# One fused attention and expert kernel: an order table with one place for each single operation, and 1e-9 brought in by a second small sum

## The chip, the cores and the metric

The kernel runs on one core of one Trainium2 chip. The metric is the device time of one execution in microseconds (us). TensorE (PE, with its weight loads PEld), VectorE (DVE), ScalarE (ACT), GpSimd (POOL) and the queue of SyncE (SP), which issues every DMA, run side by side. Each works off its own instructions in program order and waits where data or a buffer is not free.

## The reference

```python
# attention: 4 batches, 8 heads, 768 positions, 64 wide, chunks of 32 queries
scores = scale * np.matmul(q_c, k_full.transpose(0, 1, 3, 2))   # 56 keys around the chunk and 8 memory keys
scores = scores - np.max(scores, axis=-1, keepdims=True)
a = np.exp(scores)
a = a / (np.sum(a, axis=-1, keepdims=True) + 1e-09)
out[:, :, c_start:c_end] = np.matmul(a, v_full)
...
# x: (3072, 512) from the heads; w_in: 512 x 2048, w_out: 2048 x 512, handed in as float64
h = x @ w_in
P = a[0] + a[1] * h + a[2] * h2 + a[3] * h3
Q = 1.0 + np.abs(b[0]) * np.abs(h) + np.abs(b[1]) * h2
g = P / (Q + 1e-06)
return (g @ w_out).astype(np.float32)
```

## The kernel before

The 3072 tokens are six blocks of 512, and the 2048 hidden columns sixteen groups of 128. A **step** is one group of hidden columns for one block, so there are 96 steps. Each step n has a first product `g1(n)` (12 matmuls, three for each of four slices of x, because each fp32 factor is split into a high and a low part), a chain of elementwise operations on the 128x512 result h, and a second product `g2(n)` (12 matmuls into four output tiles). Steps 0 to 7 belong to block 0, steps 8 to 23 to block 1, steps 24 to 31 to block 0 again, and the blocks 2 to 5 follow. Two PSUM tiles hold h in turn, so `g1(n+2)` can start only when the chain of step n has read its h for the last time.

One letter stands for each operation in the order table. For a step: `g` first product; ACT's `s` (absolute value, then slope times it plus constant) and `i` (cubic's first line); POOL's `p` (product in the denominator); DVE's `j` (two operations, called j and J below); ACT's `t` (logarithm and exponential, t and T); DVE's `r` (three operations, r, R and Q; Q is the last to read h); POOL's `u` (high part) and `y` (low part, by a subtraction); `o` second product. For half of a weight group: `w` its DMA, ACT's `A`, DVE's `B` (a shift and a combining operation, B and C), ACT's `H` (high part), POOL's `L` (low part); 32 such halves are converted. For one of four head pairs of a block's attention: `b` scores, `m` maximum and subtraction, `x` exponential, `z` row sums, 1e-9 and reciprocal, `c` `k` transposition, `d` values, `n` division, `e` transposition back, `h` and `l` high and low part of x.

The first 31 steps, the conversion of all weights and the attention of blocks 0 to 2 stand in the string `SEQ`, written out by hand, and every engine keeps that order. Blocks 0 and 1 (`BLOCKWISE`) do their attention in PSUM tiles of 128x512 through TensorE; later blocks use a form with DVE's block transposition and DMAs. From step 31 on a loop sets the order. `RAW_SLOTS` says which piece of SBUF a weight's raw words are loaded into, `QK_SLOTS` and `V_SLOTS` which ones hold the first queries, keys and values; `CLEAR` says which engine zeroes which of these at the start; `XL_POOL` says which low parts of x POOL takes rather than DVE.

The addition of 1e-9 before the reciprocal is one DVE operation on 128x8 numbers, with a second operand `scaled` (a constant 256) in SBUF:

```python
pin(nc.vector.scalar_tensor_tensor(rinv, sums, 1e-9, scaled.broadcast_to([P, 2 * NG]), op0=ALU.add, op1=ALU.mult))
pin(nc.vector.reciprocal(rinv, rinv))
```

Of the kernel before, what the change touches and what calls it, by code (L numbers as in the profile page):

```python
# [45 lines left out]
ORDER = "i0 i1 o0 i2 i3 o1 i4 o2 i5 i6 o3 i7 o4 o5 o6 o7 i13 o13 i11 i9 i8 o8 o11 o9 i10 o10 i12 o12 i14 o14 i15 o15"  # L46
# [3 lines left out]
v02 H m03 L x03 v03 h00 Y W W d01 B l00 W c02 k02 c03 n01 w e01 z03 d02 q10 z02 n02 w k03 d03 e02 H L q11 h01 w f00  # L50
n03 A e03 l01 P h02 b10 f01 h03 A B l02 f02 w m10 B l03 f03 H x10 z10 b11 s i m11 c10 L A k10 f10 q12 j B f11 p H t
f12 r f13 v10 L x11 s u i q13 p b12 z11 c11 H k11 A g L b13 j m12 w t s w x12 A B m13 d10 p n10 i e10 v11 c12 x13 c13
r v12 H A d11 B k12 L y g w j n11 B h10 v13 H w t r d12 k13 s L e11 H d13 z12 h11 z13 l10 n12 g u A B p y i e12 A h12
w n13 j H L o t l11 w l12 w B r s L A w o B u p i w y H L A j u g B H t s L A r o w i H y g A p B j u t w s B L A y H
o p r e13 w B i g L H L j A t B w u s h13 i v21 r l13 y o j A B g p H A t r A s w i H L u j w B o g p t y r H u B A y
# [28 lines left out]
def attn_moe(ctx, tc, qk, vm, w, ab, out, seq):  # L84
# [678 lines left out]
```

## Time and profile before

| what | before |
|---|---|
| median of 3 runs | 611.65 us (611.23 to 613.16) |
| the profiled execution's own time | 611.78 us |
| its span, first to last instruction | 610.0 us |
| time outside the span | 1.78 us |
| PE busy | 587.4 us (96%) |
| DVE busy | 488.7 us (80%) |
| POOL busy | 418.2 us (69%) |
| ACT busy | 397.9 us (65%) |

The shares are means over a program whose parts differ: before about 90 us DVE and POOL are filled, after 300 us PE is. PE's granted clock is 1.00 in every stretch, which is the upper of its two levels (2.4 GHz).

### The profile page before, as it was taken

To read this page: it belongs to the slowest core of one execution; us is meant where nothing else is said; L and a number is where in the kernel's file an instruction comes from. 1 tells how busy PE (TensorE), PEld (TensorE's weight loads), DVE (VectorE), ACT (ScalarE), POOL (GpSimd) and SP (SyncE) were. 2 spreads that over 40 slices of the span, in tenths; PEclk is the share of its full clock that TensorE was granted. 3 is DMA by queue.
4 is the path that set the end of the run, shared out by engine and by line. 5 is a ranking of instruction groups with operands and counts; after the bars stand their busy time and mean duration, and the time that the engine had idled before them with its cause. 6 is when DMAs were issued, how large, how long until landed. Compare 5 with 4: busy or idle time off the path is not lost.

```text
span 610.0 us, 12743 instructions
## 1 busy us (share of the span) xinstructions
PE 587.4 (96%) x4949; PEld 474.9 (78%) x4949; DVE 488.7 (80%) x781; ACT 397.9 (65%) x638; POOL 418.2 (69%) x385
## 2 busy tenths in 40 slices
PE   7779999999999899999999999999999999999997
PEld 5556777877878687878888888888888888888886
DVE  5999999799788877898887787887788776666673
ACT  5687889778756655555575766566755656656573
POOL 3458989899855776566686676766766767676682
PEclk9999999999999999999999999999999999999999
DMA  8758332440143452522412512212320100100001
GB/s 286 302 224 319 150 138 76 167 152 21 40 115 103 139 171 87 182 70 92 135 46 75 178 35 75 73 63 83 125 71 19 35 0 19 69 2 0 1 0 70
DMA packets 34588, 61.12 MB, mean 100 GB/s; under 512 B 4192, under 2 KB 20576, under 8 KB 34144
## 3 DMA queue, kind: packets, MB, share of 16 engines
q1 hardware_dynamic: 34528, 60.31, 29.4%
q8 instruction: 39, 0.64, 0.4%
q14 instruction: 21, 0.17, 0.1%
HBM read 44.57 MB, written 7.34 MB: 85 GB/s over the span
## 4 chain that ended last, share of the span: by engine, by line
PE 73%; DVE 16%; ACT 4%; DMA 3%; issue 3%; SPq 1%; ACTq 0%; DVEq 0%
PE h L450 35%; PE o L465 34%; DVE stage L179 3%; DVE w_raw L180 3%; DVE ct L534 2%; DVE ct L521 2%; PE pairs L298 2%; PE pairs L279 2%; DMA w_raw<-in_w_dram 2%; DVE h L535 2%; SPq L137 1%; DVE ct L536 1%; DVE ct L522 1%; DMA qk<-in_qk_dram 1%; DVE rinv L312 1%
## 5 line engine op out<-in xcount | busy, mean ns | idle before, releaser
L450 PE MATMUL h<-x_hi,w_hl 128*128 128x512 f32 x768 | 240.7, 394 | 6.0 <-DVE ct L536 6.0
L465 PE MATMUL o<-w_hl,ghi 128*128 128x512 f32 x768 | 237.5, 390 | 0.7 <-ACT v_main L498 0.7
L512 POOL TENSOR_TENSOR cy<-cy,ha 128x512 f32<-128x512 f32 x96 | 124.5, 1297 | 134.2 <-ACT cy L508 133.4
L450 PEld LDWEIGHTS h<-x_hi,w_hl 128*128 128x128 f32 x768 | 141.3, 188 | 41.0 <-DVE ct L536 8.7
L465 PEld LDWEIGHTS o<-w_hl,ghi 128*128 128x128 f32 x768 | 143.6, 188 | 31.1 <-ACT v_main L498 1.2
L465 PE MATMUL o<-w_hl,glo 128*128 128x512 f32 x384 | 150.0, 391 | 0.0
L450 PE MATMUL h<-x_lo,w_hl 128*128 128x512 f32 x384 | 149.8, 390 | 0.0
L548 POOL TENSOR_TENSOR glo<-ct,ghi 128x512 fp32r<-128x512 f32 x95 | 122.8, 1293 | 6.0
L529 ACT ACTIVATE h<-cy 128x512 f32<-128x512 f32 x82 | 49.4, 602 | 102.9 <-DVE ct L522 98.0
L541 POOL TENSOR_TENSOR ghi<-ct,zero 128x512 fp32r<-128x512 f32 x95 | 98.8, 1041 | 7.7 <-DMA xf<-blocks 2.8
L521 DVE TENSOR_TENSOR ct<-ct,h 128x512 f32<-128x512 f32 x96 | 65.7, 684 | 43.1 <-ACT ct L517 42.9
L507 ACT ACTIVATE ha<-h 128x512 f32<-128x512 f32 x96 | 57.4, 598 | 62.2 <-PE h L450 61.9
L534 DVE SCALAR_TENSOR_TENSOR ct<-ct,par,h 128x512 f32<-128x512 f32 x82 | 60.7, 740 | 44.3 <-ACT h L530 44.1
L465 PEld LDWEIGHTS o<-w_hl,glo 128*128 128x128 f32 x384 | 72.1, 188 | 16.5 <-POOL glo L548 1.2
L450 PEld LDWEIGHTS h<-x_lo,w_hl 128*128 128x128 f32 x384 | 72.0, 188 | 15.6
L508 ACT ACTIVATE cy<-ha,bab 128x512 f32<-128x512 f32 x96 | 78.4, 816 | 3.3
L522 DVE SCALAR_TENSOR_TENSOR ct<-ct,par,h 128x512 f32<-128x512 f32 x96 | 71.8, 748 | 3.4
L517 ACT ACTIVATE ct<-h,par 128x512 f32<-128x512 f32 x96 | 73.2, 763 | 0.0
L536 DVE SCALAR_TENSOR_TENSOR ct<-h,ct 128x512 f32<-128x512 f32 x82 | 56.6, 691 | 2.8
L535 DVE SCALAR_TENSOR_TENSOR h<-cy,h 128x512 f32<-128x512 f32 x82 | 56.5, 688 | 0.0
L530 ACT ACTIVATE h<-h 128x512 f32<-128x512 f32 x82 | 47.7, 582 | 2.7
L192 POOL TENSOR_TENSOR w_hl<-w_raw,w_hl 128x512 fp32r<-128x512 f32 x32 | 41.9, 1316 | 5.5 <-ACT w_hl L187 5.2
(67 smaller groups left out, 463.0 us busy)
## 6 DMA issues: line engine op xcount, KB each, us to landing
w_raw<-in_w_dram SPq DMA_DIRECT2D x26, 512.0 KB, 6.2
qk_pairs<-in_qk_dram SPq DMA_DIRECT2D x16, 576.0 KB, 4.1
v_main<-in_vm_dram SPq DMA_DIRECT2D x16, 512.0 KB, 5.6
out_dram<-v_main SPq DMA_DIRECT2D x24, 256.0 KB, 2.2
qk<-in_qk_dram SPq DMA_DIRECT2D x16, 288.0 KB, 5.3
eT<-blocks SPq DMA_DIRECT2D x64, 64.0 KB, 2.1
xf<-blocks SPq DMA_DIRECT2D x64, 64.0 KB, 2.1
v_main<-in_vm_dram SPq DMA_DIRECT2D x12, 256.0 KB, 5.7
```

The source lines that it names most:

```text
L450: pin(nc.tensor.matmul(h, lhsT=wt[:, cols], rhs=xt[i][:, ct, :], start=ct == m == 0, stop=ct == NCT - 1 and m == 2))
L465: ins = nc.tensor.matmul(o, lhsT=gt[:, cols], rhs=wt, start=begin and m == 0, stop=end and m == 2)
L508: pin(nc.scalar.activation(c["y"], c["ha"], AF.Identity, scale=B1, bias=B0))
L512: pin(nc.gpsimd.tensor_tensor(c["y"], c["y"], c.pop("ha"), op=ALU.mult))
L517: pin(nc.scalar.activation(c["t"], c["h"], AF.Identity, scale=A3, bias=A2))
L521: pin(nc.vector.tensor_tensor(t, t, h, op=ALU.mult))
L522: pin(nc.vector.scalar_tensor_tensor(t, t, A1, h, op0=ALU.add, op1=ALU.mult))
L534: pin(nc.vector.scalar_tensor_tensor(t, t, A0, r, op0=ALU.add, op1=ALU.mult))
L535: pin(nc.vector.scalar_tensor_tensor(r, yy, QC, r, op0=ALU.add, op1=ALU.mult))
L536: pin(nc.vector.scalar_tensor_tensor(t, r, 2.0, t, op0=ALU.subtract, op1=ALU.mult, reverse0=True))
L541: pin(nc.gpsimd.tensor_tensor(ghi, chain[z]["t"], zero.broadcast_to([P, TB]), op=ALU.add))
L548: pin(engine.tensor_tensor(glo, chain.pop(z)["t"], gh[z].bitcast(F32), op=ALU.subtract))
```

## The change

Every operation of a chain, and each of the two DVE operations of a conversion, gets a letter of its own, so that `SEQ` can put other work between operations that stood together: s becomes s S, j becomes j J, t becomes t T, r becomes r R Q, B becomes B C, m becomes m M, and z becomes z D G. `SEQ` is written anew with these letters, and so are the order in which weights are loaded (`ORDER`), the SBUF pieces (`RAW_SLOTS`, `SPARE`) and the engines that clear (`CLEAR`). From step 31 on the split letters stand together as before. The row sums lie in one constant tile of 128 x 8 x 2 whose second column holds 1e-9. For blocks 0 and 1 a second reduction over the pair adds the two (D) and W_SCALE is divided out in the division; for later blocks ACT does the scaling and the addition. `XL_POOL` loses a unit: three low parts of x of blocks 0 and 1 fall to DVE, where it was two.

```diff
-XL_POOL = [(0, 0), (0, 1), (0, 3), (1, 0), (1, 1), (1, 2)]
+HI_ACT = []
+XL_POOL = [(0, 0), (0, 2), (1, 0), (1, 1), (1, 2)]
-CLEAR = [("qk", 0, "vv"), ("v", 2, "pp"), ("qk", 3, "va"), ("qk", 1, "pv"), ("v", 0, "aa"), ("v", 3, "vp"), ("qk", 2, "vp"), ("v", 1, "aa")]
+CLEAR = [("qk", 2, "pp"), ("v", 2, "pa"), ("v", 1, "pa"), ("qk", 0, "vv"), ("qk", 1, "pa"), ("v", 3, "pv"), ("v", 0, "vp"), ("qk", 3, "pv")]
...
-w A q00 b00 q01 v00 q02 W W b01 q03 m00 w x00 c00 k00 W W d00 m01 x01 b02 z00 c01 n00 z01 b03 e00 A m02 x02 k01 B v01
+w q00 b00 q02 A m00 q01 b02 v00 M00 m02 M02 x00 c00 q03 x02 W W b01 k00 B C W W d00 z00 D00 m01 b03 H v02 W c02 G00
...
-RAW_SLOTS = [3, 4, 10, 11, 16, 8, 14, 9, 15, 16, 12, 10, 14, 12, 15, 16]
-SPARE = 8
+RAW_SLOTS = [8, 16, 6, 13, 8, 9, 11, 15, 16, 14, 15, 12, 9, 14, 15, 16]
+SPARE = 9
...
-    scaled = const.tile([P, 1], F32, name="scaled")
-    nc.gpsimd.memset(scaled, W_SCALE)
+    small = const.tile([P, 1], F32, name="small")
+    nc.gpsimd.memset(small, W_SCALE * 1e-9)
+    sums = const.tile([P, 2 * NG, 2], F32, name="sums")
+    nc.gpsimd.memset(sums, 1e-9)
...
-        pin(nc.vector.scalar_tensor_tensor(rinv, sums, 1e-9, scaled.broadcast_to([P, 2 * NG]), op0=ALU.add, op1=ALU.mult))
+    def att_more(i, p):
+        u = unit[i, p]
+        rinv = u["rinv"] = sm.tile([P, 2 * NG], F32, name="rinv", tag="rinv")
+        if i < BLOCKWISE:
+            pin(nc.vector.tensor_reduce(rinv, sums, axis=AX.X, op=ALU.add))
+        else:
+            pin(nc.scalar.activation(rinv, sums[:, :, 0], AF.Identity, scale=W_SCALE, bias=small))
...
-        pin(nc.vector.tensor_tensor(xt, on, rinv.unsqueeze(2).broadcast_to([P, NG * 2, D]), op=ALU.mult))
+        pin(nc.vector.scalar_tensor_tensor(xt, on, 1.0 / W_SCALE, rinv.unsqueeze(2).broadcast_to([P, NG * 2, D]), op0=ALU.mult, op1=ALU.mult))
```

What the new table does on DVE is seen at the first step's chain. This is DVE's order in the kernel before: j and J of step 0 on the tile `ct_518`, one conversion's B and C, then r, R and Q.

```order
L521 TENSOR_TENSOR ct_518<-ct_518,h_430 128x512
L522 SCALAR_TENSOR_TENSOR ct_518<-ct_518,par_93,h_430 128x512
L179 TENSOR_SCALAR stage_530<-stage_530 128x512
L180 SCALAR_TENSOR_TENSOR w_raw_428<-w_raw_428,stage_530 128x512
L534 SCALAR_TENSOR_TENSOR ct_518<-ct_518,par_93,h_430 128x512
L535 SCALAR_TENSOR_TENSOR h_430<-cy_514,h_430 128x512
L536 SCALAR_TENSOR_TENSOR ct_518<-h_430,ct_518 128x512
```

Each of J, C and Q reads what the row right above it wrote. This is DVE's order in the changed kernel from the same place (L554 is j, L558 is J, L186 and L191 are B and C, L329 is the second small sum D).

```order
L186 TENSOR_SCALAR stage_504<-stage_504 128x512
L554 TENSOR_TENSOR ct_521<-ct_521,h_474 128x512
L191 SCALAR_TENSOR_TENSOR w_raw_299<-w_raw_299,stage_504 128x512
L186 TENSOR_SCALAR stage_535<-stage_535 128x512
L329 TENSOR_REDUCE rinv_544<-sums_99 128x8
L558 SCALAR_TENSOR_TENSOR ct_521<-ct_521,par_93,h_474 128x512
L191 SCALAR_TENSOR_TENSOR w_raw_485<-w_raw_485,stage_535 128x512
L186 TENSOR_SCALAR stage_568<-stage_568 128x512
L554 TENSOR_TENSOR ct_572<-ct_572,h_511 128x512
L191 SCALAR_TENSOR_TENSOR w_raw_506<-w_raw_506,stage_568 128x512
L558 SCALAR_TENSOR_TENSOR ct_572<-ct_572,par_93,h_511 128x512
```

No row here reads what the row right above it wrote; the halves of two conversions and of two steps' chains stand between one another.

The second place is block 2's attention, near step 23. In the kernel before DVE has the row sums, the addition of 1e-9 and the reciprocal of one head pair together, between Q of one step and j of the next:

```order
L536 SCALAR_TENSOR_TENSOR ct_2012<-h_1956,ct_2012 128x512
L311 TENSOR_REDUCE sums_2142<-e_1923 128x4 x2
L312 SCALAR_TENSOR_TENSOR rinv_2143<-sums_2142,scaled_97 128x8
L313 RECIPROCAL rinv_2143<-rinv_2143 128x8
L521 TENSOR_TENSOR ct_2120<-ct_2120,h_2026 128x512
```

In the changed kernel the addition has gone to ACT, and five other operations stand between the sums and the reciprocal (L577 is R, L581 is Q, L394 a block transposition):

```order
L323 TENSOR_REDUCE sums_99<-e_1904 128x4 x2
L577 SCALAR_TENSOR_TENSOR h_1891<-cy_1966,h_1891 128x512
L554 TENSOR_TENSOR ct_2015<-ct_2015,h_1986 128x512
L394 STREAM_TRANSPOSE blocks_2093<-e_1982 128x512
L581 SCALAR_TENSOR_TENSOR ct_1909<-h_1891,ct_1909 128x512
L558 SCALAR_TENSOR_TENSOR ct_2015<-ct_2015,par_93,h_1986 128x512
L335 RECIPROCAL rinv_2103<-rinv_2103 128x8
```

The third place is SP's queue at the first weights. Before, each row after the parameters (`par`) alternates between weights (`w_raw`) and the queries and keys of block 1 (`qk`):

```order
L137 DMA par_93<-in_ab_dram 128x6
L137 DMA w_raw_143<-in_w_dram 128x1024
L137 DMA qk_107<-in_qk_dram 64x1152 x2
L137 DMA w_raw_394<-in_w_dram 128x1024
L137 DMA qk_116<-in_qk_dram 64x1152 x2
L137 DMA w_raw_428<-in_w_dram 128x1024
```

In the changed kernel four weight halves stand together ahead of two loads of attention, and the row of `w_raw_577` (in-half 4) needs slot 8, from which weight 0 must first have been converted, its last reader being POOL's L for out-half 0:

```order
L145 DMA w_raw_145<-in_w_dram 128x1024
L145 DMA w_raw_299<-in_w_dram 128x1024
L145 DMA w_raw_485<-in_w_dram 128x1024
L145 DMA w_raw_506<-in_w_dram 128x1024
L145 DMA qk_109<-in_qk_dram 64x1152 x2
L145 DMA v_main0_101<-in_vm_dram 64x1024 x2
L145 DMA w_raw_577<-in_w_dram 128x1024
L145 DMA qk_128<-in_qk_dram 64x1152 x2
```

What stands behind `w_raw_577` in this queue, `qk_128` first, cannot be issued until it has been.

## Rows read from the trace of the kernel before

**Rows 1.** Busy time of each engine by stretch (us from the span's start).

```profile
core 0: us, PE busy (x) PEld busy (x) DVE busy (x) ACT busy (x) POOL busy (x), PEclk, DMA share, GB/s
...
46.00:83.40 37.40, 34.81 (x240) 26.84 (x239) 36.48 (x58) 30.16 (x53) 33.78 (x30) 1.00 0.58 217
83.40:146.60 63.20, 61.46 (x264) 48.98 (x264) 55.09 (x83) 51.90 (x87) 55.68 (x47) 1.00 0.32 117
146.60:231.00 84.40, 82.54 (x900) 66.25 (x900) 69.60 (x117) 52.66 (x85) 59.38 (x54) 1.00 0.34 105
231.00:300.00 69.00, 68.28 (x793) 55.37 (x781) 59.12 (x101) 40.12 (x63) 43.91 (x41) 1.00 0.34 104
300.00:600.00 300.00, 300.00 (x2226) 246.22 (x2225) 229.21 (x360) 187.75 (x295) 204.14 (x182) 1.00 0.17 53
```

**Rows 2.** PE in order of time: first products of steps 4 and 8.

```profile
start us, us, engine line op out<-in xcount [idle before <-releaser]
54.44 0.73 PE L450 MATMUL h<-x_hi,w_hl 128*128 128x512 f32 x2 [0.52 <-DVE ct L536]
...
83.44 0.73 PE L450 MATMUL h<-x_hi,w_hl 128*128 128x512 f32 x2 [0.32 <-DVE ct L536]
```

**Rows 3.** PE in order of time: first product of step 19.

```profile
146.62 0.72 PE L450 MATMUL h<-x_hi,w_hl 128*128 128x512 f32 x2 [0.31 <-DVE ct L536]
```

**Rows 4.** The chain that ended last, two products late in the span (start, us, what).

```profile
505.64 2.72 PE o L465 x12
508.36 2.72 PE h L450 x12
```

**Rows 5.** DVE in order of time, six neighbours (C, l, m, M, B, C).

```profile
27.12 0.70 DVE L180 SCALAR_TENSOR_TENSOR w_raw<-w_raw,stage 128x512 uint32<-128x512 uint32 x1
27.72 0.69 DVE L431 TENSOR_TENSOR x_lo<-pa,x_hi 128x512 fp32r<-128x512 f32 x1
28.33 0.69 DVE L342 TENSOR_REDUCE mx<-pa 128x8 f32<-128x512 f32 x1
29.06 0.69 DVE L345 TENSOR_TENSOR e<-pa,mx 128x512 f32<-128x512 f32 x1
29.66 0.69 DVE L179 TENSOR_SCALAR stage<-stage 128x512 uint32<-128x512 uint32 x1
30.39 0.70 DVE L180 SCALAR_TENSOR_TENSOR w_raw<-w_raw,stage 128x512 uint32<-128x512 uint32 x1
```

**Rows 6.** Busy time of L312 (1e-9 and scale) by stretch.

```profile
core 0: us, DVE busy (x), PEclk, DMA share, GB/s
8.00:60.00 52.00, 4.24 (x8) 1.00 0.78 289
180.00:300.00 120.00, 5.56 (x8) 1.00 0.38 117
```

**Rows 7.** DVE in order of time: L312 and the reciprocal of the first head pair.

```profile
13.02 0.17 DVE L312 SCALAR_TENSOR_TENSOR rinv<-sums,scaled 128x8 f32<-128x8 f32 x1
13.22 0.20 DVE L313 RECIPROCAL rinv<-rinv 128x8 f32<-128x8 f32 x1
```

**Rows 8.** All engines in order of time: L312 of the seventh pair, and POOL.

```profile
54.90 1.28 POOL L548 TENSOR_TENSOR glo<-ct,ghi 128x512 fp32r<-128x512 f32 x1
...
55.01 1.20 DVE L312 SCALAR_TENSOR_TENSOR rinv<-sums,scaled 128x8 f32<-128x8 f32 x1
```

**Rows 9.** POOL in order of time: p of step 2 (44.73), u, L, y, p, u, and p of step 8.

```profile
44.73 1.26 POOL L512 TENSOR_TENSOR cy<-cy,ha 128x512 f32<-128x512 f32 x1
...
68.10 1.03 POOL L541 TENSOR_TENSOR ghi<-ct,zero 128x512 fp32r<-128x512 f32 x1
69.10 1.31 POOL L192 TENSOR_TENSOR w_hl<-w_raw,w_hl 128x512 fp32r<-128x512 f32 x1
70.37 1.27 POOL L548 TENSOR_TENSOR glo<-ct,ghi 128x512 fp32r<-128x512 f32 x1
71.61 1.29 POOL L512 TENSOR_TENSOR cy<-cy,ha 128x512 f32<-128x512 f32 x1
72.87 1.03 POOL L541 TENSOR_TENSOR ghi<-ct,zero 128x512 fp32r<-128x512 f32 x1
...
88.81 1.30 POOL L512 TENSOR_TENSOR cy<-cy,ha 128x512 f32<-128x512 f32 x1 [1.54 <-ACT cy L508]
```

**Rows 10.** DMA issues by line: count, size of one, median us to landing.

```profile
w_raw<-in_w_dram SPq DMA_DIRECT2D x26, 512.0 KB, 6.2
```

More of the change, by code (lines that the diff above doesn't have):

```diff
@@ L51 @@
[L51 to L55, printed above, removed]
@@ L63 @@
+J S o p g
 """
@@ L501, in attn_moe, with state, chain_slope @@
     spares = []
+    def state(x):
+        return chain.setdefault(x, {"h": hps[x]})
     def chain_abs(x):
-        c = chain[x] = {"h": hps.pop(x)}
-        c["y"] = room(tp, "cy", F32, "cy", 2)
+        c = state(x)
         c["ha"] = room(tp, "ha", F32, "ha", 1)
         pin(nc.scalar.activation(c["ha"], c["h"], AF.Abs))
+    def chain_slope(x):
+        c = chain[x]
+        c["y"] = room(tp, "cy", F32, "cy", 2)
         pin(nc.scalar.activation(c["y"], c["ha"], AF.Identity, scale=B1, bias=B0))
@@ L514, in chain_line, with chain_square, chain_cube, chain_ln @@
     def chain_line(x):
-        c = chain[x]
+        c = state(x)
         c["t"] = room(tp, "ct", F32, "ct", 3)
         pin(nc.scalar.activation(c["t"], c["h"], AF.Identity, scale=A3, bias=A2))
-    def chain_above(x):
+    def chain_square(x):
         t, h = chain[x]["t"], chain[x]["h"]
         pin(nc.vector.tensor_tensor(t, t, h, op=ALU.mult))
+    def chain_cube(x):
+        t, h = chain[x]["t"], chain[x]["h"]
         pin(nc.vector.scalar_tensor_tensor(t, t, A1, h, op0=ALU.add, op1=ALU.mult))
-    def chain_inverse(y):
+    def chain_ln(y):
         r = chain[y]["h"]
@@ L529, in chain_inverse, with chain_exp, chain_error, chain_mend @@
         pin(nc.scalar.activation(r, chain[y]["y"], AF.Ln, bias=QC))
+    def chain_exp(y):
+        r = chain[y]["r"]
         pin(nc.scalar.activation(r, r, AF.Exp, scale=-1.0))
     def chain_ratio(y):
-        yy, t, r = chain[y].pop("y"), chain[y]["t"], chain[y].pop("r")
+        t, r = chain[y]["t"], chain[y]["r"]
         pin(nc.vector.scalar_tensor_tensor(t, t, A0, r, op0=ALU.add, op1=ALU.mult))
+    def chain_error(y):
+        yy, r = chain[y].pop("y"), chain[y]["r"]
         pin(nc.vector.scalar_tensor_tensor(r, yy, QC, r, op0=ALU.add, op1=ALU.mult))
+    def chain_mend(y):
+        t, r = chain[y]["t"], chain[y].pop("r")
         pin(nc.vector.scalar_tensor_tensor(t, r, 2.0, t, op0=ALU.subtract, op1=ALU.mult, reverse0=True))
@@ L539, in chain_hi @@
         ghi = gh[z] = room(gp, "ghi", F32R, "ghi", 2) if z < total - 4 else room(at, "ghi", F32R, "xf", 2)
-        if z < total - 1:
+        if z < total - 1 and z not in HI_ACT:
             pin(nc.gpsimd.tensor_tensor(ghi, chain[z]["t"], zero.broadcast_to([P, TB]), op=ALU.add))
@@ L590, in attend @@
                 else:
-                    pieces[kind](i, p)
+                    for name in dict(m="mM", z="zDG").get(kind, kind):
+                        pieces[name](i, p)
     warm = ps_h.tile([P, 512], F32, name="warm", tag="h")
@@ L685, in attn_moe @@
         chain_abs(n)
+        chain_slope(n)
         chain_below(n)
@@ L690, in attn_moe @@
             evac(*done_block, [0, 1])
-        chain_above(n)
+        chain_square(n)
+        chain_cube(n)
         attend(n, "czm")
-        chain_inverse(n)
+        chain_ln(n)
+        chain_exp(n)
         if done_block:
@@ L696, in attn_moe @@
         chain_ratio(n)
+        chain_error(n)
+        chain_mend(n)
         chain_hi(n - 1)
@@ L701, in attn_moe @@
     assert all(n < LAST for n, kind in att)
-    count.update(dict.fromkeys("spijtr", LAST - 1), g=LAST, u=LAST - 2, y=LAST - 2, o=LAST - 3)
+    count.update(dict.fromkeys("sSpijJtTrRQ", LAST - 1), g=LAST, u=LAST - 2, y=LAST - 2, o=LAST - 3)
     for token in FINAL.split():
```

75 lines of the change are left out of this document (48 added, 27 removed).

## The prediction, made before the changed kernel ran

> **What bounds the kernel now.** I read the busy time by stretch first. After 300 us PE is busy for all of 300.00 us [rows 1], and the chain that ended last consists there of products of 2.72 us in an unbroken row [rows 4]. So a step costs 2 x 2.72 = 5.44 us, and nothing that the change does on another engine can shorten that part. From 46.0 to 83.4 us it is different: DVE is busy for 36.48 of 37.40 us and POOL for 33.78, while PE has holes [rows 1]. The first products of steps 4 and 8 start at 54.44 and 83.44 us, both released by DVE [rows 2]; four steps took 29.0 us instead of 21.8. DVE is the bound there, with POOL close behind. From 83.4 to 146.6 us, step 8 to step 19 [rows 2, 3], eleven steps took 63.2 us, where 11 x 5.44 = 59.8; PE shows only 1.74 us idle [rows 1], so a hole costs about twice its length, because the matmuls behind it have to fill the pipeline again. By that factor the holes of 146.6 to 231 us (84.40 - 82.54 = 1.86) cost 3.7 us and those of 231 to 300 us (0.72) cost 1.4 [rows 1]. From step 8 on a better order can so give 3.4 + 3.7 + 1.4 = 8.5 us at most; what it gives ahead of step 8 is up to DVE and POOL.
>
> **DVE's neighbours.** The six rows on DVE all last 0.69 or 0.70 us, but they don't start at equal distances [rows 5]. Where an operation reads what the one before it wrote, the distance is 0.73 (m to M, B to C); where it doesn't, 0.60 or 0.61 (C to l, l to m, M to B). A dependent neighbour costs 0.12 us more. Counted over both orders up to Q of step 6, whose end lets step 8's first product start, the kernel before has 46 dependent neighbours and the changed one 12: 34 x 0.12 = 4.1 us less on DVE. Both orders hold the same sixteen converted halves and eight head pairs up to there.
>
> The Trainium skill speaks against this. Its page "VectorE: DVE Perf Modes", section "The DRAIN you can't avoid", says that the next operation does not start until the pipe of the one before is empty, and that chaining without semaphores saves nothing. By that page the distance would not depend on the order and this term would be zero; the rows just named show two distances, so I go by them and keep that page's case as a rival.
>
> **The small sum.** L312 handles eight numbers per partition, yet took 4.24 us in the first eight instances [rows 6]. With POOL idle it took 0.17 us [rows 7]; the instance at 55.01 us took 1.20 and ended at 56.21, just when POOL's subtraction ended (54.90 + 1.28 = 56.18) [rows 8]. It reads two tiles of SBUF, and waits for POOL's operation to end. D, which replaces it on DVE, reads one. Its cost isn't in the trace: bounded below by 0.17 [rows 7] and above by what L312 took, 4.24 / 8 = 0.53 [rows 6]. I take 0.2, near the reciprocal of as many numbers [rows 7], because it has one input only: 4.24 - 8 x 0.2 = 2.6 us saved (bounds 0 to 2.9). The division gets a factor and with it another form; both forms take 0.69 to 0.70 us [rows 5], so it costs nothing. The third low part of x on DVE adds 0.6 [rows 5].
>
> The Trainium skill's page "SBUF — State Buffer", section "Who interferes with whom", states that a VectorE instruction with two SBUF inputs waits for a GpSimd instruction that reads SBUF, and that a reduction never does on trn2. The first half agrees with the 1.20 us row; no run here shows the second yet.
>
> **Early sum.** DVE up to Q6: -4.1 - 2.6 + 0.6 = -6.1 us. Two other queues then have to be asked.
> PE: from step 4's first product it works through four first and five second products and one transposition of 0.6 before step 8's: 9 x 2.72 + 0.6 = 25.1 us. Step 4 waits for Q of step 2. Up to that Q the new order has 20 dependent neighbours fewer (-2.4) and cheaper small sums (-1.6), but two more row sums, one more division and a low part of x stand ahead (+2.4): -1.6, so 54.4 - 1.6 = 52.8, and step 8 at 77.9 instead of 83.4 [rows 2]: -5.5.
> POOL: an L, y or p costs 1.24 to 1.27 us, a u 1.00, by the distances of starts [rows 9]. From p of step 2 to p of step 8 it now has 9 L, 6 p, 6 y, 6 u and two low parts of x: 23 x 1.25 + 6 x 1.00 = 34.8 us, where 44.1 us passed (44.73 to 88.81) [rows 9], since four conversions and one low part of x, there inside, now come before. Its start I put 1.5 us later, an estimate, since 3.5 us more of other DVE work (by the counts and distances above) stands ahead of Q of step 0. Then p of step 8 comes at 46.2 + 34.8 = 81.0 instead of 88.8: -7.8.
> PE's own bound, -5.5, is the tightest. Three nearly full queues will also wait for one another now and then: I take **-5.0** for step 8 (bounds -2.0 and -6.1).
>
> **Later terms.** Steps 8 to 19: a cycle of two steps is g (2.72), s, S, i, j, J, t, T, r, R and Q, and few of these neighbours part in the new order here; POOL's part of a step is 1.26 + 1.00 + 1.24 = 3.5 us, and with the 11 conversions that its new order has in steps 8 to 15 it needs (8 x 3.5 + 11 x 1.27) / 8 = 5.25 us a step [rows 9], just under PE's 5.44. Of the 3.4 us I take **-1.0** (0 to -3.4).
> Steps 19 to 31: four instances of L312 leave DVE, 5.56 / 8 = 0.70 us each [rows 6], 2.8 in all, and the reciprocal stands five operations behind its sums, so that ACT's small operation hides (the trace doesn't show it: 0.17 as for eight numbers on DVE, at most the 0.70 of L312) behind them. If that cover were gone, DVE would wait that long per pair, no more than now. I take **-2.0** of 3.7 (0 to -3.7).
> From 231 us, where DVE waits for ACT between sums and reciprocal: **-0.5** of 1.4 (0 to -1.4).
> After 300 us: nothing; PE hides the rest.
> Clearing: POOL zeroes the second half of the first values as its sixth region, so their load and all behind it in SP's queue are issued some 2.5 us later (three more regions of 0.6 to 0.95 us); the order has their readers later by as much, and I cost it at nothing. Without that cover DVE would start that much later: +2.5, inside the -2.0 bound above.
> Sum: -5.0 - 1.0 - 2.0 - 0.5 = -8.5. The span goes from 610.0 to 601.5 us, and with 1.78 us outside it the execution takes 603.3. The profiled execution of before stands 0.13 us above the median of the runs, which is within their spread.
>
> **The rivals.**
> POOL becomes the bound. It is busy for 33.78 of 37.40 us already, and its holes there sum to 3.6 [rows 1]. If its queue keeps those holes, p of step 8 comes at 81.0 + 3.6 = 84.6, 4.2 earlier, less the half microsecond for each of the two following steps that inherit it: -3.2; with half of the later terms -5.0: 606.8. For it speaks that a step with two conversions costs it 3.5 + 2 x 1.27 = 6.0 us, more than PE's 5.44; against it, that conversions have been brought forward.
> The distance doesn't follow the order (the case of the Trainium skill's page on VectorE). The 4.1 is lost: DVE up to Q6 -2.0, later terms as taken less half of the first: -2.0 - 0.5 - 2.0 - 0.5 = -5.0, again about 606.8. The 0.60 and 0.73 of equal operations speak against it [rows 5], but m and B always stand ahead of the same reader, so it could be a matter of the kinds.
> Slower: SP's queue. In-half 4 may be loaded only when POOL's L of out-half 0 has ended, and a landing takes 6.2 us (median) [rows 10]. DVE's B of that half stands ahead of Q of step 0, and block 1's queries wait in SP behind the load. It is needed at about 39 us and I expect the slot free at 34, so that 5 us pass if the queue is short. Each microsecond beyond goes into Q0 and all that follows. If the slot came free at 46 us (L waits on ACT, which waits for step 0's product, which waits for four units of attention), the load would land at 52: 13 late, less 8.5: 616. It outweighs the gains if the slot comes free after 41 us. Against it: by the count of DVE's new order no more than 21 us of its work stands ahead of step 0's last slice of x, and the queue starts that work near 9 us.
> The change does nothing that can be measured: the gain at step 8 is eaten by a wait of block 1's readers: 610 to 613.
>
> **How the numbers follow.** A difference under 0.3% of 611.65 (609.8 to 613.5) can't be told from none. Forecast (600 to 606) 0.60; better than it, PE unbroken from step 4 on (610.0 - 6.1 - 3.4 - 3.7 - 1.4 + 1.78 = 597.2 at the best) 0.10; POOL as the bound 0.11; equal distances 0.05; no change 0.08; slower 0.06. The first four are faster: 0.86. The range runs from 597.2, a little rounded up to 597.5, to where no change begins, 609.8.
>
> **What would show it.** Right: step 8's first product near 78 us; small sums near 0.2 us even beside POOL; distances of 0.60 after B, j and m where something else follows; step 32's first product near 223. Wrong: DVE idle between 35 and 50 us with a DMA or ACT as releaser; D as long as POOL's operation; POOL without holes from 46 to 85 and PE waiting for its y or L.

## The result, and the profile after

The changed kernel takes 606.79 us (median; 605.13 to 608.00 in 4 runs) against 612.10 us for the kernel before beside it (611.23 to 613.16): ratio 0.991, 95% interval 0.988 to 0.994. It is faster and inside the range, but 3.5 us above the number forecast and 0.8 us outside the band of 600 to 606 us, to which the forecast gave a chance of 0.60. The profiled execution is the fastest of the four: 605.13 us, span 603.0 us, 7.0 us less than the span before. The time outside the span is 2.13 us, where it was 1.78.

From the page of the changed kernel: busy time by engine, and the chain that ended last by engine.

```profile
PE 585.9 (97%) x4949; PEld 475.9 (79%) x4949; DVE 467.7 (78%) x765; ACT 396.7 (66%) x651; POOL 418.6 (69%) x388
...
PE 82%; DMA 5%; DVE 5%; POOL 4%; issue 2%; ACT 1%; SPq 1%; POOLq 0%; ACTq 0%; DVEq 0%
```

DVE was busy for 488.7 us and stood on 16% of that chain; now it is 467.7 us and 5%. The stretches that answer to [rows 1] (the borders lie where the steps now lie):

```profile
core 0: us, PE busy (x) PEld busy (x) DVE busy (x) ACT busy (x) POOL busy (x), PEclk, DMA share, GB/s
...
46.00:77.00 31.00, 30.62 (x199) 24.62 (x193) 28.67 (x50) 27.81 (x48) 29.65 (x27) 1.00 0.56 205
77.00:140.00 63.00, 61.08 (x270) 49.73 (x269) 56.24 (x86) 52.55 (x89) 58.48 (x50) 1.00 0.36 126
140.00:224.00 84.00, 82.78 (x857) 66.36 (x863) 63.73 (x111) 52.73 (x88) 58.16 (x52) 1.00 0.35 105
224.00:293.00 69.00, 68.89 (x844) 55.92 (x840) 56.20 (x97) 40.52 (x67) 44.20 (x42) 1.00 0.34 104
```

Between steps 3 and 8 PE is busy for 30.62 of 31.00 us, where it was busy for 34.81 of 37.40. DVE is no longer full (28.67); POOL nearly is (29.65). The first products that answer to [rows 2, 3], in order of time on PE:

```profile
52.51 0.73 PE L477 MATMUL h<-x_hi,w_hl 128*128 128x512 f32 x2
...
78.30 0.71 PE L477 MATMUL h<-x_hi,w_hl 128*128 128x512 f32 x2
...
140.89 0.62 PE L477 MATMUL h<-x_hi,w_hl 128*128 128x512 f32 x2
```

None of them waits for DVE any more. Step 8 comes 5.1 us earlier than before, step 19 5.7, step 32 6.4 (224.66 against 231.06), the end 7.0.

DVE, POOL and SP in order of time around step 1 (L329 is the small sum D, L191 C, L186 B, L558 J, L554 j):

```profile
32.13 0.68 DVE L191 SCALAR_TENSOR_TENSOR w_raw<-w_raw,stage 128x512 uint32<-128x512 uint32 x1
...
32.73 0.69 DVE L186 TENSOR_SCALAR stage<-stage 128x512 uint32<-128x512 uint32 x1
32.75 1.31 POOL L203 TENSOR_TENSOR w_hl<-w_raw,w_hl 128x512 fp32r<-128x512 f32 x1 [3.10 <-ACT w_hl L198]
...
33.33 0.16 DVE L329 TENSOR_REDUCE rinv<-sums 128x8 f32<-128x16 f32 x1
33.41 0.73 DVE L558 SCALAR_TENSOR_TENSOR ct<-ct,par,h 128x512 f32<-128x512 f32 x1
...
34.02 1.28 POOL L545 TENSOR_TENSOR cy<-cy,ha 128x512 f32<-128x512 f32 x1
34.06 0.68 DVE L191 SCALAR_TENSOR_TENSOR w_raw<-w_raw,stage 128x512 uint32<-128x512 uint32 x1
34.09 0.33 SPq L145 DMA_DIRECT2D w_raw<-in_w_dram  x1
...
34.47 1.11 SPq L145 DMA_DIRECT2D qk<-in_qk_dram  x2
34.66 0.69 DVE L186 TENSOR_SCALAR stage<-stage 128x512 uint32<-128x512 uint32 x1
...
35.26 0.68 DVE L554 TENSOR_TENSOR ct<-ct,h 128x512 f32<-128x512 f32 x1
```

B starts, and 0.60 us later the next operation, where C used to start after 0.73 [rows 5]. The prediction left open whether that is a matter of the kinds of operation. Seven rows a little later answer it (L432 is a division n, L372 M, L577 R, L581 Q, L573 r):

```profile
38.44 0.68 DVE L432 SCALAR_TENSOR_TENSOR xt<-pa,rinv 128x512 f32<-128x512 f32 x1
39.04 0.68 DVE L372 TENSOR_TENSOR e<-pa,mx 128x512 f32<-128x512 f32 x1
39.63 0.68 DVE L577 SCALAR_TENSOR_TENSOR h<-cy,h 128x512 f32<-128x512 f32 x1
40.23 0.69 DVE L186 TENSOR_SCALAR stage<-stage 128x512 uint32<-128x512 uint32 x1
40.83 0.68 DVE L581 SCALAR_TENSOR_TENSOR ct<-h,ct 128x512 f32<-128x512 f32 x1
41.43 0.68 DVE L191 SCALAR_TENSOR_TENSOR w_raw<-w_raw,stage 128x512 uint32<-128x512 uint32 x1
42.02 0.74 DVE L573 SCALAR_TENSOR_TENSOR ct<-ct,par,h 128x512 f32<-128x512 f32 x1
```

M, R, Q and C all start 0.59 to 0.60 us after a row that wrote nothing they read. In the same trace, up to 140 us, the ten J that stand right behind their own j start 0.71 to 0.72 us after it, and seven that stand behind an operation of like length on something else 0.60. So it is what is read, not the kind. D takes 0.16 us in the middle of a POOL operation that runs from 32.75 to 34.06; L312 took 1.20 us in that situation [rows 8]. In-half 4 is issued by SP at 34.09; the prediction expected its slot free at 34.

One new hole is the change's own. POOL, ACT, DVE and PE in order of time at step 8 (L554 and L558 are j and J of step 8, L536 its s, L545 its p, L593 is y of step 6, L550 i of step 8):

```profile
81.40 0.78 ACT L550 ACTIVATE ct<-h,par 128x512 f32<-128x512 f32 x1
...
83.44 0.68 DVE L554 TENSOR_TENSOR ct<-ct,h 128x512 f32<-128x512 f32 x1
...
84.15 0.75 DVE L558 SCALAR_TENSOR_TENSOR ct<-ct,par,h 128x512 f32<-128x512 f32 x1
...
84.93 0.60 ACT L536 ACTIVATE ha<-h 128x512 f32<-128x512 f32 x1 [2.75 <-DVE ct L558]
...
86.46 1.28 POOL L545 TENSOR_TENSOR cy<-cy,ha 128x512 f32<-128x512 f32 x1 [2.97 <-ACT cy L541]
...
87.70 1.27 POOL L593 TENSOR_TENSOR glo<-ct,ghi 128x512 fp32r<-128x512 f32 x1
...
89.03 0.50 PE L492 MATMUL o<-w_hl,glo 128*128 128x512 f32 x1 [1.79 <-POOL glo L593]
```

s only reads h, and ACT's i, which stands before it and reads h too, started at 81.40; but s waits 2.75 us for J, which only reads h too. p is late by it, y stands behind p in POOL's queue, and PE stands still for 1.79 us in the middle of step 6's second product. A second hole is longer, 2.98 us, where PE waits for the normalisation n that DVE starts at 38.44:

```profile
39.17 0.66 PE L442 MATMUL pa<-ident,xt 128*128 128x128 f32 x4 [2.98 <-DVE xt L432]
```

### The profile page after: what moved, and what is told of

Its sections match the earlier page's. It is cut to its first block, busy times and chain, and to the rows that moved or that the text cites. A ratio compares the mean times of both kernels' runs of the same rounds, so it can differ in the third digit from the quotient of the medians.

```text
span 603.0 us, 12757 instructions
## 1 busy us (share of the span) xinstructions
PE 585.9 (97%) x4949; PEld 475.9 (79%) x4949; DVE 467.7 (78%) x765; ACT 396.7 (66%) x651; POOL 418.6 (69%) x388
## 4 chain that ended last, share of the span: by engine, by line
PE 82%; DMA 5%; DVE 5%; POOL 4%; issue 2%; ACT 1%; SPq 1%; POOLq 0%; ACTq 0%; DVEq 0%
PE h L477 39%; PE o L492 38%; DMA w_raw<-in_w_dram 3%; PE pairs L312 2%; PE pairs L290 2%; POOL w_hl L203 1%; DMA v_main<-in_vm_dram 1%; DMA xf<-blocks 1%; POOL glo L593 1%; DMA qk_pairs<-in_qk_dram 1%; PE pa L421 1%; SPq L145 1%; DVE ct L558 0%; DVE ct L573 0%; DVE ct L581 0%
## 5 line engine op out<-in xcount | busy, mean ns | idle before, releaser
L545 POOL TENSOR_TENSOR cy<-cy,ha 128x512 f32<-128x512 f32 x96 | 124.5, 1297 | 131.8 <-ACT cy L541 118.9
L593 POOL TENSOR_TENSOR glo<-ct,ghi 128x512 fp32r<-128x512 f32 x95 | 122.8, 1292 | 6.2
L573 DVE SCALAR_TENSOR_TENSOR ct<-ct,par,h 128x512 f32<-128x512 f32 x82 | 61.1, 746 | 51.6 <-ACT h L569 51.3
L554 DVE TENSOR_TENSOR ct<-ct,h 128x512 f32<-128x512 f32 x96 | 65.7, 684 | 45.4 <-ACT ct L550 42.4
L536 ACT ACTIVATE ha<-h 128x512 f32<-128x512 f32 x96 | 57.3, 597 | 59.9 <-PE h L477 56.3
L550 ACT ACTIVATE ct<-h,par 128x512 f32<-128x512 f32 x96 | 73.4, 766 | 2.3 <-PE h L477 2.3
L558 DVE SCALAR_TENSOR_TENSOR ct<-ct,par,h 128x512 f32<-128x512 f32 x96 | 71.6, 746 | 2.9
L581 DVE SCALAR_TENSOR_TENSOR ct<-h,ct 128x512 f32<-128x512 f32 x82 | 56.5, 689 | 2.6
L577 DVE SCALAR_TENSOR_TENSOR h<-cy,h 128x512 f32<-128x512 f32 x82 | 56.4, 688 | 0.0
```

What stands on the lines that cost most here:

```text
L536: pin(nc.scalar.activation(c["ha"], c["h"], AF.Abs))
L545: pin(nc.gpsimd.tensor_tensor(c["y"], c["y"], c.pop("ha"), op=ALU.mult))
L550: pin(nc.scalar.activation(c["t"], c["h"], AF.Identity, scale=A3, bias=A2))
L554: pin(nc.vector.tensor_tensor(t, t, h, op=ALU.mult))
L558: pin(nc.vector.scalar_tensor_tensor(t, t, A1, h, op0=ALU.add, op1=ALU.mult))
L573: pin(nc.vector.scalar_tensor_tensor(t, t, A0, r, op0=ALU.add, op1=ALU.mult))
```

## The experiments

Each ratio is to the kernel before beside it. A difference between two of these kernels is known to within some 2 us, by the intervals. The chain's and the conversion's second operations (J, R and Q, C) and the subtraction M are "put back" when they stand right behind their firsts again.

**The order without the small sum.** The changed tables with the old addition of 1e-9 and the old division.

```diff
-            pin(nc.vector.tensor_reduce(rinv, sums, axis=AX.X, op=ALU.add))
...
+        pin(nc.vector.scalar_tensor_tensor(rinv, sums[:, :, 0], 1e-9, scaled.broadcast_to([P, 2 * NG]), op0=ALU.add, op1=ALU.mult))
```

> The new tables with the old arithmetic: 1e-9 and the factor 256 are again one operation of DVE with two tiles of SBUF, for all 24 head pairs, at the place of the small sum. Theory (small sum and order each give a part): DVE waits for POOL again, 4 us up to step 8 of which 2 to 3 reach PE; step 8's first product near 80.5, the span 2 to 4 us above the changed kernel's 603.0. Rival (the order alone made the gain, the small sum hides in DVE's new slack): the span within 1 us of 603.0.

608.50 us, ratio 0.994 (0.991 to 0.996): 1.7 us slower than with the sum, a little less than expected, and near the edge of what the intervals can tell. The group of the old operation in this kernel comes first; then, in the changed kernel, what ACT does in its place for the later blocks, and D on DVE. The three numbers are shortest, median and longest in ns:

```profile
L328 DVE SCALAR_TENSOR_TENSOR rinv<-sums,scaled x8: 156/608/962, 13.8 to 56.3; 128x8 f32<-128x8 f32 x8
```

```profile
L331 ACT ACTIVATE rinv<-sums,small x16: 284/301/303, 170.1 to 474.7; 128x8 f32<-128x8 f32 x16
L329 DVE TENSOR_REDUCE rinv<-sums x8: 157/161/172, 13.8 to 52.4; 128x8 f32<-128x16 f32 x8
```

With one SBUF input in place of two, the spread is gone. From 8 to 60 us the eight take 1.30 us in place of 4.09 in this kernel and 4.24 before [rows 6].

**The small sum without the order.** The tables of before (J, R, Q, C, M, D, G right behind their firsts), the new operations.

```diff
-w q00 b00 q02 A m00 q01 b02 v00 M00 m02 M02 x00 c00 q03 x02 W W b01 k00 B C W W d00 z00 D00
...
+w A q00 b00 q01 v00 q02 W W b01 q03 m00 M00 w x00 c00 k00 W W d00 m01 M01 x01 b02 z00 D00 G00 c01 n00 z01 D01
...
```

> The small sum and ACT's scaling with all tables of before (order, slots, clearing, low parts of x). Theory: DVE, which is filled up to step 8 there, gets 2.6 us back, the later parts about 1: span 606 to 607.5. Rival (the order alone made the gain): 609 to 610.

610.75 us, ratio 0.996 (0.995 to 0.998): by the interval 1 to 3 us faster, between what the theory (2.5 to 4) and the rival (0 to 1) expected. Order (-3.8) and sum (-1.6) add up to what both give (-5.3).

**All second operations put back.** Changed kernel, only their places in the order.

```diff
-... f10 C P q12 z11 B i f11 s j C c10 A ... A J C i
+... f10 P q12 z11 B C i f11 s j J c10 A ... A i
```

> The changed kernel, but each second operation of DVE stands right behind its first again (J behind j, R and Q behind r, C behind B, M behind m); all other places stay. Theory (a dependent neighbour costs 0.12 us and DVE was the bound): some 30 dependent neighbours more up to step 8, 3.5 us more DVE work, of which 1.5 to 3.5 reach the span: 604.5 to 606.5. Rival (the distances only matter where DVE is full, and it no longer is): within 0.7 us of 603.0.

611.76 us, ratio 1.000 (0.998 to 1.002): 5.0 us lost, more than expected and all that the change had gained. It still has the small sum, which alone gave 1.6; so with the neighbours back, nothing else that is new in the tables shows a gain.

**Only the conversion and the attention put back (C, M).**

```diff
-... k00 B C W W d00 ... n02 B k01 h00 C
+... k00 B C W W d00 ... n02 B C k01 h00
```

> Changed kernel with only the conversion's second VectorE operation and the attention's subtraction put right behind their firsts again; the chain's operations stay apart. By the order, 32 dependent neighbours stand on VectorE up to step 7's last chain operation (13 in the changed kernel, 41 with all put back). Theory (VectorE's own time): 19 more neighbours at 0.12 us are 2.3 us; step 8 at 80.2 to 81.0, step 32 at 226.5 to 227.5, median 608.5 to 609.8. Rival (the conversion is not on the path; all the loss of 5 us with everything back comes of the chain): step 8 within 0.7 us of 78.3 and the median 606 to 607.3.

611.29 us, ratio 0.999 (0.997 to 1.001): 4.5 us lost, more than either expectation.

**Only the chain put back (J, R, Q).**

```diff
-... s j C c10 A f12 B H v10 D11 f13 S b12 A J C i
+... s j J C c10 A f12 B H v10 D11 f13 S b12 A C i
```

> Changed kernel with only the chain's second product and its two error operations put right behind their firsts again; conversion and attention stay apart. By the order, 28 dependent neighbours up to step 7's last chain operation, against 13. Theory (VectorE's own time): 15 more at 0.12 us are 1.8 us; step 8 at 79.6 to 80.6, step 32 at 226 to 227, median 608.0 to 609.3; together with the run with the conversion put back about the 5 us that both cost. Rival (what counts is when the chain's results come, its operations now wait for POOL's and ScalarE's in VectorE's queue): step 8 at 82 or later with VectorE idle over 1 us more than in the changed kernel, median 610 to 612.

609.99 us, ratio 0.995 (0.993 to 0.997): 3.2 us lost. The expectations counted dependent neighbours to step 7 only. Over the whole table of 31 steps the changed order has 53, the chain put back 81, the conversion 86, all 105; by 0.12 us each (0.73 - 0.60) that is 3.4, 4.0 and 6.2 us, and 3.2, 4.5 and 5.0 were measured. This count came after the results; the shorter ones in the expectations were exceeded by all three.

To see where the time goes, here are the distances of first products in the traces (us; the last column is time at half clock between 30 and 60 us):

```
kernel             step 1   1 to 8   8 to 10  10 to 19  19 to 32   half clock
before              31.88    51.57    11.02    52.16     84.43      0
changed             30.03    48.27    13.45    49.13     83.77      0
order alone         32.08    50.52    14.45    49.28     83.67      3.4
sum alone           30.95    49.65    11.01    52.14     86.21      0
all put back        32.01    51.63    13.12    50.38     84.74      6.8
conversion back     31.91    50.14    14.80    49.91     84.89      3.4
chain back          30.44    51.92    14.71    49.00     83.85      6.8
all back, filled    32.45    50.04    13.14    50.39     86.10      0
low part first      29.29    48.98    13.47    49.12     83.02      3.4
old clears          30.75    49.33    13.90    49.82     83.80      3.4
s ahead of j        33.48    50.28    11.05    48.96     83.05      8.2
s, norm earlier     29.19    50.84    11.04    48.96     84.24      6.8
```

Step 1 comes anywhere from 29.19 to 33.48 us in the profiled executions of this table, although little of the order ahead of it differs among the changed tables. Kernels with the same order up to step 8 (changed, low part first, old clears, s ahead of j) take 48.27 to 50.28 us from step 1 to step 8, so a single trace tells such a stretch to 2 us.

The count does not come out stretch by stretch. The chain put back has 15 more dependent neighbours up to Q of step 8, worth 1.8 us, and loses 3.65 us from step 1 to step 8 and 1.26 to step 10; behind step 10, with some 14 more, it loses nothing. Step 8 comes at 82.36 us, where the expectation's rival put it. DVE is busy there for 47.55 of 51.92 us, in the changed kernel for 45.63 of 48.27: 1.9 us more work, as counted, and 1.7 us more waiting. But s ahead of j, with the changed kernel's order up to there, has 45.78 of 50.29, so the work hardly scatters and the waiting does. The neighbours' own time is shown, then, but not that it is the whole of the loss.

**Low part of step 6 ahead of p of step 8 on POOL.**

```diff
-... w J s S p A H B t g T y A C
+... w J s S y p A H B t g T A C
```

> The changed kernel, but POOL's low part y of step 6 stands ahead of p of step 8 instead of behind it. In the changed kernel POOL idles for 2.97 us ahead of that p while y could run, and PE idles for 1.79 us in the second product of step 6 for it. Theory (a head-of-line wait in POOL's queue): the hole of PE closes and the span falls by 1.8 to 3 us. Rival (p of step 8 comes later by y's 1.25 us and so does the chain of step 8): no gain, or PE waits two steps on instead.

606.90 us, ratio 0.991 (0.987 to 0.994): nothing. PE's hole moved to the next first product, in order of time on PE:

```profile
91.73 0.50 PE L477 MATMUL h<-x_hi,w_hl 128*128 128x512 f32 x1 [2.27 <-DVE ct L581]
```

There it waits for Q of step 8: the chain of that step is late, wherever y stands.

**s of step 8 ahead of its j.**

```diff
-... r R i Q j w J s S p A H B t
+... r R i Q s j w J S p A H B t
```

> One token moves against the changed kernel: step 8's absolute value (ScalarE, reading the step's PSUM bank h) stands ahead of that step's two VectorE products, which read the same bank; in the changed kernel it stands behind them, started at 84.93 and waited 2.75 us for the second of them. Theory: reads of one bank by two engines go in the order of the program, so the wait is the order's own. Then the absolute value starts near 82.2, GpSimd's product of step 8 (88.81 in the changed kernel's trace or near it) comes 1 to 2 us earlier, the hole of 1.79 us inside the second products of step 6 closes to under 0.5, step 10's first product comes at 90.0 to 90.8 (91.75 before the move) and the median falls by 1 to 1.8 us (605.0 to 605.8). Rival: the wait only changes sides, VectorE's first product of step 8 now waits for the absolute value or GpSimd is late by its own queue; hole and step 10 within 0.3 us of where they were, median within 0.5.

603.72 us, ratio 0.986 (0.982 to 0.989): 3.1 us faster than the changed kernel, more than expected. Neither ACT's nor DVE's own order changes by this move, only which of the two is ahead. ACT and POOL in order of time (step 8 starts at 83.77 in this trace):

```profile
87.54 0.59 ACT L536 ACTIVATE ha<-h 128x512 f32<-128x512 f32 x1
...
89.06 1.30 POOL L545 TENSOR_TENSOR cy<-cy,ha 128x512 f32<-128x512 f32 x1
```

No wait for J is left, p starts 5.3 us after the step's first product instead of 8.2, and steps 8 to 10 take 11.05 us instead of 13.45. The intervals of the two ratios touch, but three kernels with the move (this one, and below the normalisation earlier and the hole filled) have medians of 603.3 to 604.2, and three without it (changed, low part first, old clears) 606.8 to 607.4.

**The same at step 1, and the normalisation earlier.** s ahead of j, the normalisation n of unit (1,0) ahead of J, r, R and Q of step 0 earlier.

```diff
-... t j L C J G11 q13 T c11 m12 s d10 S r H n10 M12 R p e10 ...
+... t c11 d10 s j L C n10 J T r G11 q13 R m12 S H Q M12 p e10 ...
```

> The move of step 8 and, at step 1, where TensorE has its longest hole (2.98 us up to 39.17, waiting for the normalisation of attention unit (1,0) on VectorE, which starts at 38.44 though the sums' reciprocal ended at 37.3 and the values at 36.2): the normalisation stands ahead of step 1's second product, step 0's error term ahead of it too, and step 1's absolute value ahead of step 1's products. Theory: the hole is this one place in VectorE's order; the normalisation starts at 36.5 to 37.1, the hole falls to 0.8 to 1.6, and steps 2 to 4 start 1 to 2 us earlier (step 2 at 40 to 40.7, step 4 at 51 to 51.5); against the first move alone the median falls by another 0.8 to 1.8. Rival: from 26 to 46 us VectorE is busy 19.3 of 20 us, so its sum sets step 4 whatever stands first; what is moved ahead makes step 1's chain late by the same; hole smaller, but step 4 within 0.4 us of 52.5 and the median within 0.5 of the first move alone.

605.96 us, ratio 0.989 (0.987 to 0.992): no faster than with step 8's move alone, and by the median 2.2 us slower. DVE and PE in order of time:

```profile
36.34 0.69 DVE L554 TENSOR_TENSOR ct<-ct,h 128x512 f32<-128x512 f32 x1 [1.33 <-ACT ha L536]
...
42.12 1.93 PE L354 MATMUL pa<-qk 128*32 128x128 f32 x32 [3.19 <-DVE e L372]
```

Now j waits 1.33 us for s: the wait has changed sides. The subtraction M (L372) has slid behind the chain, and PE has a second hole of 3.19 us for it.

**Only the normalisation earlier,** with step 8's move.

```diff
-... T c11 m12 s d10 S r H n10 M12 R p e10 ...
+... T c11 d10 n10 m12 s S r H M12 R p e10 ...
```

> The kernel with step 8's absolute value moved (603.7 us), and on VectorE only the normalisation of attention unit (1,0) two places earlier, ahead of a maximum and of step 0's error term, so that TensorE's hole of 2.98 us before step 2 is cut in two: some 1.8 us before the normalisation's transpositions, and the rest behind them, since step 2's first product still waits for step 0's last VectorE operation, which stays where it is. Theory (VectorE's sum sets step 2, not the hole's place): step 2's first product 11.4 to 12.4 us after step 1's, as in the changed kernel (11.6), and the median within 0.8 of 603.7, although the shorter idle stretches may leave the clock at full speed. Rival one (the hole itself is what is lost): step 2 comes 10.3 to 10.8 us after step 1 and the median is 602.0 to 602.9. Rival two (the clock is what is lost): no stretch at half clock from 30 to 60 us, and the median 1 to 2 us lower, though step 2 comes no earlier.

603.28 us, ratio 0.985 (0.983 to 0.988): the fastest median, not told apart from the move alone. PE in order of time:

```profile
37.08 0.66 PE L442 MATMUL pa<-ident,xt 128*128 128x128 f32 x4 [1.72 <-DVE xt L432]
39.93 1.94 PE L354 MATMUL pa<-qk 128*32 128x128 f32 x32 [2.19 <-DMA qk<-in_qk_dram]
```

The hole is cut in two and the two together are longer: behind the normalisation PE waits for block 1's queries, whose load SP issues right behind in-half 4 (34.47 in the changed kernel). The granted clock fell here too, at 38.4 us for 6.8. Step 2 comes 12.6 us after step 1 (11.6 in the changed kernel).

**The hole filled, to keep the clock.** 14 thrown-away transpositions in the hole of 2.98 us, with step 8's move; then 26 of them in the hole of 5.0 us of the kernel with all put back.

```diff
+        if (i, p) == (1, 0):
+            for _ in range(14):
+                pin(nc.tensor.transpose(out=xp[:, :P], in_=ident, identity=ident))
```

> The kernel with step 8's absolute value moved, and 14 transpositions of the identity (thrown away: the real ones overwrite them) on TensorE ahead of attention unit (1,0)'s transpositions, in the hole of 2.98 us before step 2. Each takes 0.165 us in the rows, 2.3 us in all. In that kernel's trace the granted clock falls to half at 41.6, inside the hole, and stays there for 6.8 us; the changed kernel's profiled execution kept the full clock, its other runs had a mean clock of 0.991 to 0.992. Theory: it is TensorE's idleness there that lowers the clock, and the slow stretch costs 1 to 2.5 us: no stretch at half clock between 36 and 50 us, mean clock 0.996 or more in most runs, median 601.2 to 602.7 against 603.7. Rival: in the slow stretch TensorE waits for the others anyway, or the clock falls whatever stands in the hole: median within 0.6 of 603.7, or above it by the time that the last transposition keeps the real ones waiting.

> The changed kernel with all second operations right behind their firsts again (28 more dependent neighbours by step 7, 3.4 us by the rows; it lost 5.0 us), and 26 thrown-away transpositions (4.3 us) in its hole of 5.0 us before step 2. Theory: what goes beyond the neighbours' own time is the clock, which falls to half for 6.8 us in that longer hole; filled, the median falls by 1 to 2.5 us, to 609.3 to 610.8. Rival: the excess is waiting in VectorE's queue and the clock's stretch is hidden behind it; median within 0.6 of 611.8.

604.16 us, ratio 0.987 (0.985 to 0.990), and 611.52 us, ratio 0.999 (0.998 to 1.001): neither median differs from that of the kernel without the filling by more than noise, as both rivals had it. In the first the clock of the profiled execution fell all the same, from 43.2 us for 3.4; the hole there is down to 1.30 us. Stretches (PEclk 1.00 is 2.4 GHz, 0.50 is 1.2) of the kernel with all put back, then of the filled one:

```profile
37.00:41.00 4.00, 1.09 (x33) 0.81 (x32) 3.89 (x8) 3.50 (x7) 1.90 (x3) 0.87 0.99 339
41.00:45.00 4.00, 1.86 (x20) 1.48 (x24) 3.93 (x8) 3.48 (x8) 3.74 (x6) 0.50 0.88 312
```

```profile
37.00:41.00 4.00, 3.94 (x59) 3.50 (x58) 3.90 (x8) 3.51 (x7) 2.01 (x2) 1.00 0.89 296
41.00:45.00 4.00, 2.00 (x42) 1.56 (x40) 3.93 (x7) 3.96 (x9) 3.63 (x5) 1.00 0.99 353
```

The clock stays at its higher level in the filled one, and steps 1 to 8 take 50.04 us in place of 51.63. But other executions of it had slow stretches elsewhere (the profiled one from 7.8 to 14.6 us). Its five executions with a mean clock of 0.999 or more have a median of 610.3 us, its six others 612.4.

**The old list of clears.** Changed kernel, `CLEAR` of before.

> The changed kernel with the old list of which engine clears which buffer, in the old order, at the start. The prediction costed the new list at nothing, with 2.5 us to either side. Theory: the clears lie beside the first transfers; median 606.0 to 607.6 (606.8 with the new list), step 1's first product within 0.8 us of the changed kernel's. Rival: VectorE's and ScalarE's first operations come later by clears that GpSimd does in the new list; step 1 and the median 1 to 2.5 us later.

607.43 us, ratio 0.992 (0.990 to 0.994); step 1 at 30.75 us. The list is worth nothing that shows.

## Why the prediction was right, and where it was off

**The number.** The measured 606.79 us lies outside the forecast's own band of 600 to 606, and just on the 606.8 us that two rivals were priced at, POOL as the bound and equal distances. The median alone would speak for them. The rows rule out equal distances (below), and POOL was held by a wait and not by its load (below), so that the number meets theirs is chance.

**What bound the kernel: right.** DVE stood on the path up to step 8, and a part of what DVE lost there came off the time.

**DVE's neighbours: right.** Operations behind B, j and m follow at 0.60 us when they read something else. Undoing it costs 5.0 us, and its two parts 4.5 and 3.2. The two parts together exceed the whole; each is known to some 2 us, and why they do was not settled. The rival of equal distances falls by the 0.60 and 0.73 in the rows above, for the same kinds of operation. The Trainium skill's page "VectorE: DVE Perf Modes", section "The DRAIN you can't avoid", does not quite say what the prediction took from it: it lets an operation start earlier when nothing holds it. So the two distances in the traces don't go against it.

**The small sum: mechanism right, size right for DVE.** 1.30 us for eight; predicted 8 x 0.2. That is 2.9 us of DVE's time up to 60 us; the median got 1.6 to 1.7 us, and where the rest went is open. The Trainium skill's page "SBUF — State Buffer", section "Who interferes with whom", says that a reduction never waits for GpSimd on this chip; that half, which nothing could show before, is now borne out: D takes 157 to 172 ns in all eight places, in the middle of a POOL operation too.

**Step 8, -5.0: measured -5.1, but partly by chance.** From step 1 to step 8 the gain is 3.3 us, and 1.3 to 2.6 in the traces of the three other kernels with the same order up to there, which had slow stretches of the clock. The other 1.8 is an earlier step 1, and step 1 scatters by over 4 us among like kernels. The prediction's sum for DVE (-6.1) is not reached. From step 1 to step 8 DVE is busy for 45.63 us in place of 50.25, 4.6 less, but it now waits there where it hardly did: the longest wait is 1.10 us at 58.62, of a j for the s of its step. PE has a hole of 2.98 us before step 2 (step 2 itself comes 3.2 us later than before, and step 4 1.9 earlier), through which DVE works without a pause; cutting it in two or filling it gained nothing that shows.

**POOL, p of step 8 at 81.0: wrong.** It came at 86.46, later even than the 84.6 of the rival with POOL as the bound, and PE waited for POOL's y, which the prediction had named as a sign of being wrong. But POOL stood idle for 2.97 us just before, and with the same work in POOL's queue the wait of PE is gone when s stands ahead of j. The prediction asked POOL's queue only for its own work; what held it was s standing behind J.

**Steps 8 to 19, -1.0: measured -0.6, made of two unforeseen things.** Steps 10 to 19 gain 3.0 us, down to 49.13, where nine steps at PE's 5.44 are 48.96; and steps 8 to 10 lose 2.4 by the hole in step 6's second product. One token in front of another gives the 2.4 back: 11.05 us, as before.

**Steps 19 to 31, -2.0: the step that failed, measured -0.7.** The prediction took DVE's freed time (2.8 us) as time of PE, and reckoned that each hole costs twice its length. DVE's busy time did fall, from 69.64 to 64.31 us between the first products of steps 19 and 32, but PE's idle time only from 1.84 to 1.22. These are PE's longest holes there, before and then after:

```profile
200.28 0.72 PE L465 MATMUL o<-w_hl,ghi 128*128 128x512 f32 x2 [0.74 <-ACT v_main L498]
209.89 0.73 PE L450 MATMUL h<-x_hi,w_hl 128*128 128x512 f32 x2 [1.03 <-DVE ct L536]
```

```profile
171.81 0.86 PE L290 MATMUL pairs<-qk_pairs 64*32 64x64 f32 x64 [0.61 <-DMA qk_pairs<-in_qk_dram]
218.21 0.73 PE L477 MATMUL h<-x_hi,w_hl 128*128 128x512 f32 x2 [0.58 <-DVE ct L581]
```

Only one of the two before was a wait for DVE; after, half of it is left, and a wait for block 2's queries has come. The order alone, with the old operation on DVE, has 83.67 us there, as much as the changed kernel (83.77), and kernels with the same order here lie between 83.02 and 84.61; so a gain from the small operation's move to ACT does not show in this stretch. Nor does the factor of two: 0.62 us less idle gave 0.66 here, and 0.61 less gave 0.6 in the 69 us from step 32 on. From step 10 to 19 it nearly held (1.71 us less, 3.0 gained). The prediction laid it to matmuls that fill the pipeline again; the rows show the first pair behind a hole at 0.73 us in place of 0.62, and what else a hole costs is open.

**From step 32, -0.5: measured -0.6.** **The clears, 0: right.** **SP's queue: right** that the slot is free at 34 and nothing is lost to that load. It is next in line, though: block 1's queries behind it are what PE waits for once the normalisation comes earlier.

**The median against the profiled execution.** By the terms, span 601.5 was forecast and 603.0 profiled; the other three executions had spans of 604.6 to 605.9 and a mean clock of 0.991 to 0.992, against 1.000. So 1.5 us of the 3.5 are the terms above. Another 0.35 is time outside the span, which the prediction took as unchanged: it is 2.10 to 2.19 us in every execution of the changed kernel, of the order alone and of low part first, and 1.9 or less in all other kernels here, for a reason not known. (So some 0.35 us of the 3.1 that the move of s gained is not in the span either.) The remaining 1.7 is that the profiled execution was the quickest, with an early step 1 and without a slow stretch. How much of that is the clock and how much the start was not settled.

## What to carry to other kernels

On an engine that is full, count the neighbours of which the second reads what the first wrote, and put something independent between them: here each cost the engine 0.12 us, and putting all 52 back cost 5.0 us. The count gives the engine's own time; what reaches the end also depends on the waits that the new order makes or ends. A tiny operation with two SBUF inputs took up to 1.20 us here beside GpSimd, and 0.17 without; look at its longest instance, not its median. When operations get places of their own, order those that share a PSUM tile across engines as well: a reader placed behind another engine's reader waited for it here, and one token moved was worth about 3 us.

## What the runs showed of the hardware that was not expected

**Two engines that only read the same PSUM tile ran in the order of the program.** s on ACT waited 2.75 us for J on DVE in the changed kernel; with s in front at step 8 the wait is gone, and at step 1 it turned into 1.33 us of DVE waiting for s. The Trainium skill's page "PSUM — Partial Sum Buffer", section "PSUM bank collisions raise a hardware error", says that the compiler's scheduler adds a dependency between instructions of different engines that touch the same bank and quadrant, reads and writes alike. The two waits agree with that; what put them into this program is open, and what happens without them wasn't tried.

**TensorE's clock after a hole.** In the changed kernel's relatives with holes of 1.3 to 5.0 us before step 2, the granted clock fell to 1.2 GHz in or soon behind the hole, for 3.4 or 6.8 us, in ten of twelve profiled executions. It stayed at 2.4 GHz in the changed kernel's own, behind 2.98 us, and in the one with all put back and filled, behind 2.00. Of 74 executions of the kernel before beside the experiments, on four chips, the 26 with a mean clock of 0.999 or more have a median of 611.4 us, the 48 others 612.9. That is a difference of 1.5 us within one kernel (95% interval 0.9 to 2.1). It shows that slow stretches and longer times go together; the filled holes did not show in the median that this one place causes it.
